# Retention and soft mixture of experts on one core: the second expert layer and the results in parts of 256, 128 and 128 columns instead of two parts of 256

## The chip, the core and the metric

The kernel runs on one core of a Trainium2 chip. The core has a matrix engine (TensorE, PE in the profile; its weight loads are a row of their own, PEld), VectorE (DVE), ScalarE (ACT), GpSimd (POOL) and a sequencer that issues DMAs here (SyncE, SP). All data is float32. The metric is the device time of one execution in microseconds.

## The reference, cut to what matters

```python
def _attn_ref(q, k, v):                      # B, H, S, D = 8, 8, 576, 64
    scores = scale * np.matmul(q, k.transpose(0, 1, 3, 2))
    ...                                      # decay by gamma ** (i - j), lower triangle
    return np.matmul(scores * Dmat, v)
def _moe_ref(x, phi, w1, w2):                # N, D, E, 4, F = 4608, 512, 8, 4, 1024
    logits = x @ phi                         # 32 slots: 8 experts of 4
    d = softmax(logits, axis=0)
    slot_input = (d.T @ x).reshape(E, 4, D)
    for e in range(E):
        slot_out[e] = np.maximum(slot_input[e] @ w1[e], 0.0) @ w2[e]
    c = softmax(logits, axis=1)
    return c @ slot_out.reshape(32, D)       # the result, 4608 x 512
```

The last two lines of work are the ones that the change touches: the second expert layer (times `w2`) and the final product of the combine weights `c` with the 32 slot outputs.

## The kernel before, in words

**Stages.** The 4608 tokens are 36 tiles of 128. A loop over the tiles computes retention, keeps the transposed results, and gathers the first softmax over groups of four tiles; W1 and W2 are loaded behind it in units of 128x1024 (512 KB), 41 of them into slots `ws`. Then come the first expert layer (L572) and the second one (`expert_2`), and the results. The order on every engine is the order of the code: the schedule is manual, and each engine takes its instructions in that order.

**W2 in two parts.** `PARTS` divides the 512 columns of W2, of the slot outputs and of the result into two parts of 256. One call `expert_2(k, n)` is a step: four matmuls (L626) of one expert and one half of the hidden units, side by side on four groups of 32 output partitions, that add into one accumulator `pp2[k]`, a piece of the PSUM bank `pm`. Part k takes 16 steps. The operands are plain float32, and each such matmul stands in the profile as two MATMUL records.

**Slot outputs.** `slot_out(k, fill)` copies the accumulator to SBUF (ACT, L632), adds the pieces of the experts up with one matmul by the selection matrix `delta` (L635, PE), writes the sum rounded (ACT, L636) and the remainder of the rounding for the upper 64 rows (DVE, L637) into `so`. Two calls in `fill` put other work on the engines between these steps.

**Results.** `final(k, b)` makes columns of part k for group b, four token tiles: four matmuls (L651) of 128 rows by 256 columns in the rounded type float32r, one MATMUL record each, with the four combine tiles `ct[b]` as weights and `so` as moving data; two copies of 128x512 out of PSUM by `evac`, which gives them to ACT (L611) and DVE (L613) in turn; and one DMA of 512 KB on SP's queue (L660; two of 256 KB at L655 for the first group). The PSUM banks `po` of these results are four that go round, and some of the combine tiles use them too. The buffers of the results are the free slots and W2 slots that have been read, in the list `stg`.

**Combine tiles.** `stack_c(g)` makes `ct[g]` with four transposes (L537) and one copy, on DVE (L543) for even g and on ACT (L545) for odd g.

**Order at the end.** 16 steps of part 0, `slot_out(0)` with the first two combine tiles and three steps of part 1 in it, then for eight groups: `final(0, b)`, the combine tile of group b + 2, and `STEPS[b]` steps of part 1 (2, 2, 2, 2, 2, 2, 1, 0). Then `slot_out(1)` with `final(0, 8)` in it, and the nine groups of part 1 with nothing between them. SP issues the DMAs of the results in the order in which `final` is called, and each waits for the two copies of its group.

Of the kernel before, what the change touches and what calls it, by code (L numbers as in the profile page):

```python
# [15 lines left out]
P = 128  # L16
NP = H // 2
DM = H * D
NE, NSE, F = 8, 4, 1024
NS = NE * NSE  # L20
NCH = 4
NT = 36
NG = NT // 4
# [3 lines left out]
NR = 6  # L27
CST = ((0, 64), (64, NP * 64), (64 * (NP + 1), (NCH + 1) * H), (64 * (NP + 1) + (NCH + 1) * H, (NCH + 1) * NP))
NCST = 64 * (NP + 1) + (NCH + 1) * (H + NP)
STEPS = (2, 2, 2, 2, 2, 2, 1, 0, 0)  # L30
ACT_STACKS = (3, 5, 6, 7)
PARTS = ((0, 256), (256, 512))


def tile_order():
    order = []
    for b0 in range(0, B, 2):
        for c in range(NCH):
            order.append((b0, c))
            order.append((b0 + 1, c))  # L40
        order.append((b0, NCH))
    return order
# [3 lines left out]
def retention_softmoe(ctx, tc, tok, phi, wun, cst, gtab, msel, out):  # L46
    nc = tc.nc
# [41 lines left out]
    unit_tile = {}  # L89
# [266 lines left out]
    for t in range(NT):  # L356
# [37 lines left out]
        if late and t:  # L394
            x, y = late.pop(0)
# [26 lines left out]
    def pbank():  # L422
        return ps_o.tile([P, 512], F32, name="po")
# [55 lines left out]
    for i in range(4):  # L479
        nc.tensor.matmul(pr[i * NS:(i + 1) * NS, 0:1], lhsT=en[:, i * NS:(i + 1) * NS],  # L480
                         rhs=tri[:, 63:64], start=True, stop=True, skip_group_check=True)
# [3 lines left out]
    for z in range(2):  # L485
        for i in range(4):
            nc.tensor.matmul(pph[z][i * NS:(i + 1) * NS, 0:256], lhsT=en[:, i * NS:(i + 1) * NS],
                             rhs=xN[4 * g + i][:, 2 * z:2 * z + 2], start=True, stop=True,
                             skip_group_check=True)
        if z == 0:  # L490
# [3 lines left out]
            out=acc[:, z * 256:(z + 1) * 256], in0=acc[:, z * 256:(z + 1) * 256], scalar=alpha,  # L494
# [36 lines left out]
    def stack_c(g, eng=nc.vector):  # L531
        if eng is nc.vector:
            pc = ps_n.tile([P, NP, P], F32R, name="pn")
        else:
            pc = pbank4().bitcast(F32R)
        for i in range(4):
            nc.tensor.transpose(pc[:, i, :], cs[g][:, i].rearrange("p r w s -> p (r w s)"), identr)  # L537
        if g < NR:
            c = ring.tile([P, NP, P], F32R, name="x")
        else:  # L540
            c = ctw[g - NR]
        if eng is nc.vector:
            nc.vector.tensor_copy(out=c, in_=pc)  # L543
        else:
            nc.scalar.copy(out=c, in_=pc)  # L545
        ct[g] = c
# [19 lines left out]
    for n in range(8):  # L566
        nh, eh, kp = n // 4, n // 2 % 2, n % 2
        for c in range(2):
            for i in range(4):
                w = unit_tile[(0, 4 * eh + i, nh, kp)]  # L570
                w = w[c] if isinstance(w, tuple) else w[:, c * 512:(c + 1) * 512]
                nc.tensor.matmul(p1[nh][i * NS:(i + 1) * NS, :], lhsT=sim[kp][:, c, 4 * eh + i, :],  # L572
                                 rhs=w, start=(n % 4 == 0 and c == 0),
# [3 lines left out]
        for i in range(4 if n != 2 else 0):  # L577
            w = unit_tile[(0, 4 * eh + i, nh, kp)]
# [7 lines left out]
        if n == 2:  # L586
            hm = [slots.tile([P, 1024], F32, name="kv3").rearrange("p (c e s) -> p c e s", c=4, e=NE)]
# [11 lines left out]
        if n in (5, 6):  # L599
            for i in (free[1:3], free[3:6])[n - 5]:  # L600
                x = slots.tile([P, 2, 4, 2, 2, NS], F32R, name=f"ws{i}")
# [4 lines left out]
    stg = [ws[i] for i in free[6:]]  # L606
    ev = [0]

    def evac(o, i):
        if ev[0] % 2 == 0:  # L610
            nc.scalar.copy(out=o, in_=i)  # L611
        else:
            nc.vector.tensor_copy(out=o, in_=i)  # L613
        ev[0] += 1

    pp2 = {}

    def expert_2(k, n):
        lo, hi = PARTS[k]
        fh, e = divmod(n, NE)  # L620
        if n == 0:
            pp2[k] = pm[:, 0:hi - lo]
        u = unit_tile[(1, e, k, fh)]
        w = u.rearrange("p (c f) -> p c f", c=4)
        for i in range(4):
            nc.tensor.matmul(pp2[k][i * NS:(i + 1) * NS, :], lhsT=hm[fh][:, i, e, :], rhs=w[:, i, :],  # L626
                             start=(n == 0), stop=(n == 2 * NE - 1), skip_group_check=True)
        stg.append(u)

    def slot_out(k, fill):  # L630
        lo, hi = PARTS[k]
        nc.scalar.copy(out=p2s[:, lo:hi], in_=pp2[k])  # L632
        fill[0]()
        pso = ps_n.tile([P, NP, P], F32, name="pn").rearrange("p a i -> p (a i)")[:, 0:hi - lo]
        nc.tensor.matmul(pso, lhsT=delta, rhs=p2s[:, lo:hi], start=True, stop=True)  # L635
        nc.scalar.copy(out=so[:, lo:hi], in_=pso)  # L636
        nc.vector.tensor_tensor(out=so[64:P, lo:hi], in0=pso[64:P], in1=so[64:P, lo:hi].bitcast(F32),  # L637
                                op=ALU.subtract)
        fill[1]()

    def final(k, b):
        lo, hi = PARTS[k]
        w = hi - lo
        o = stg.pop(0)
        stg.append(o)
        o = o[:, 0:4 * w].rearrange("p (c f) -> p c f", c=4)
        n = 512 // w
        for c0 in range(0, 4, n):
            po = pbank().rearrange("p (c f) -> p c f", c=n)
            for c in range(c0, c0 + n):  # L650
                nc.tensor.matmul(po[:, c - c0, :], lhsT=ct[b][:, c, :], rhs=so[:, lo:hi],  # L651
                                 start=True, stop=True)
            evac(o[:, c0:c0 + n, :], po)
            if k == 0 and b == 0:
                nc.sync.dma_start(  # L655
                    out=out[0, :, c0 * w:(c0 + n) * w].rearrange("p (c f) -> p c f", c=n),
                    in_=o[:, c0:c0 + n, :])
        if k == 0 and b == 0:
            return
        nc.sync.dma_start(out=out[k * NG + b].rearrange("p (c f) -> p c f", c=4), in_=o)  # L660

    for n in range(2 * NE):
        expert_2(0, n)
        if n == 1:
            hidden_out(1)
        if n in (3, 5, 7, 9):
            split_c(n // 2 + 4)
# [2 lines left out]
        stack_c(0)  # L670
        stack_c(1, nc.scalar)

    def fill_1():
        for n in range(3):
            expert_2(1, n)

    slot_out(0, (fill_0, fill_1))
    n = 3
    for b in range(NG - 1):
        final(0, b)  # L680
        if b + 2 < NG:
            stack_c(b + 2, nc.scalar if b % 2 else nc.vector)
        for _ in range(STEPS[b]):
            expert_2(1, n)
            n += 1
    slot_out(1, (lambda: final(0, NG - 1), lambda: None))
    for b in range(NG):
        final(1, b)
    man.close()


# [21 lines left out]

def unpack(o):
    import numpy as np
    o = o.reshape(2, NG, P, 4, 256).transpose(1, 3, 2, 0, 4).reshape(NT, P, DM)
    y = np.empty((B, S, DM), o.dtype)
    for t, (b, c) in enumerate(tile_order()):
        if c < NCH:
            y[b, c * P:(c + 1) * P] = o[t]  # L720
        else:
            y[b:b + 2, NCH * P:] = o[t].reshape(2, 64, DM)
    return y.reshape(B * S, DM)
# [72 lines left out]
```

## Time and profile before

| | us |
|---|---|
| time, median of 3 runs (range) | 234.79 (234.09 to 235.82) |
| time of the profiled execution | 233.35 |
| span of the profiled execution | 231.6 |
| first result matmul of part 0 | 199.6 |
| first result matmul of part 1 | 215.9 |
| last copy of a result out of PSUM ends | 223.0 |
| SP's last wait, for the result DMAs, ends | 230.5 |

The times in the span count from its start. PE is busy for 215.7 us of it (93%), DVE for 130.4, ACT for 82.4, POOL for 62.5. The DMA engines move 72.54 MB, of which 9.44 MB are the results. In the profile a group of instructions is one line with its count, its busy time and the mean duration of one; a matmul's duration covers its way through the array, so the distance between the starts of two matmuls is shorter than the duration of one. The granted TensorE clock of the run is 0.984 on average, and 1.00 in the windows from 200.7 to 223.0 us.

### The profile page before, as it was taken

The page shows a single profiled execution, that of the slowest core. Times are in us where ns is not written, and L with a number is a line of the kernel's source. Part 1 is how long each engine was busy: PE and PEld are TensorE (multiplying, and loading weights), DVE is VectorE, ACT ScalarE, POOL GpSimd, SP SyncE. Part 2 cuts the span into 40 slices and gives each one's busy share as a digit, 9 for nine tenths or more (in the row PEclk, how much of TensorE's full clock was granted, in tenths as well). Part 3 has the DMA queues.
Part 4 walks back from the last instruction along what each step waited for, and adds up shares of the span by engine and source line. Part 5 has one row for each costly group of instructions (what it writes and reads, how often), then busy time and mean ns, then how long its engine had stood idle before and what let it go on. Part 6 is the DMA issues. An engine that isn't in the chain of part 4 may idle for free.

```text
span 231.6 us, 9098 instructions
## 1 busy us (share of the span) xinstructions
PE 215.7 (93%) x3971; PEld 159.7 (69%) x3971; DVE 130.4 (56%) x302; ACT 82.4 (36%) x198; POOL 62.5 (27%) x72
## 2 busy tenths in 40 slices
PE   8789999999999999999999999999899999999730
PEld 8678877777886886787887787887763245666620
DVE  0365645766756767746847855864764132446740
ACT  2231542452443433442352352353131142444730
POOL 2743414334233333515313531440100110000000
PEclk9999999999999999999999999999999999999985
DMA  7999898789899799899789998887573899666897
GB/s 228 392 382 325 317 339 303 253 327 403 282 333 378 260 311 381 311 343 335 257 297 363 345 380 297 293 296 248 181 276 126 326 415 408 256 246 267 356 404 290
DMA packets 23511, 72.54 MB, mean 313 GB/s; under 512 B 2608, under 2 KB 2992, under 8 KB 23472
## 3 DMA queue, kind: packets, MB, share of 16 engines
q1 hardware_dynamic: 23184, 71.51, 84.1%
q8 instruction: 31, 0.51, 0.9%
q10 hardware_dynamic: 288, 0.46, 0.6%
q14 instruction: 8, 0.07, 0.1%
HBM read 62.52 MB, written 9.44 MB: 311 GB/s over the span
## 4 chain that ended last, share of the span: by engine, by line
PE 89%; DVE 4%; ACT 2%; issue 1%; DVEq 0%
PE px L234 14%; PE pss L195 13%; PE pn L263 8%; PE pst L255 7%; PE px L222 7%; PE pn L180 7%; PE pm L626 6%; PE pm L277 5%; PE pm L325 4%; PE po L651 4%; PE pst L572 3%; PE pn L572 3%; PE px L131 2%; DVE sT L200 2%; DVE sT L203 1%
## 5 line engine op out<-in xcount | busy, mean ns | idle before, releaser
L155 POOL TENSOR_TENSOR kv<-kv,cst 128x512 f32<-128x512 f32 x36 | 37.5, 1042 | 85.0 <-DMA kv<-in_tok 72.4
L241 DVE TENSOR_TENSOR x<-px,gb 128x512 f32<-128x512 f32 (+1 forms) x37 | 24.9, 675 | 31.9 <-PE px L234 30.9
L234 PE MATMUL px<-sT,kv 128*64 128x128 f32 x576 | 38.6, 275 | 2.6 <-DVE sT L203 1.8
L200 DVE TENSOR_TENSOR sT<-pss,cst 64x256 f32<-64x256 f32 x72 | 30.3, 421 | 10.9 <-PE pss L195 8.5
L181 ACT COPY kt<-pn 128x512 f32<-128x512 f32 x36 | 21.1, 587 | 40.7 <-PE pn L180 40.7
L234 PEld LDWEIGHTS px<-sT,kv 128*64 128x64 f32 x576 | 30.9, 137 | 4.6 <-PE pst L255 2.3
L265 ACT COPY x<-pn 128x512 f32<-128x512 f32 x33 | 19.3, 585 | 36.7 <-PE pn L263 36.6
L195 PE MATMUL pss<-qs,kt 64*64 64x64 f32 (+1 forms) x1152 | 31.6, 247 | 0.7 <-ACT kt L181 0.7
L195 PEld LDWEIGHTS pss<-qs,kt 64*64 64x64 f32 x1152 | 26.1, 133 | 6.9 <-issue 4.6
L255 PEld LDWEIGHTS pst<-kv 128*64 128x64 f32 x512 | 17.5, 137 | 10.1 <-issue 7.9
L180 PE MATMUL pn<-ident,kv 128*128 128x128 f32 x144 | 22.7, 280 | 0.4 <-DMA kv<-in_tok 0.4
L203 DVE TENSOR_TENSOR sT<-pss,cst 128x512 f32<-128x512 f32 x32 | 22.1, 692 | 0.9
L255 PE MATMUL pst<-kv 128*64 128x64 f32 x512 | 21.9, 228 | 0.0
L263 PE MATMUL pn<-ident,x 128*128 128x128 f32 x132 | 21.7, 287 | 0.1
L163 POOL TENSOR_TENSOR gb<-g,cst 128x512 f32<-128x512 f32 x16 | 16.6, 1040 | 10.9 <-DVE x L241 10.9
L222 PE MATMUL px<-qs,sb 64*64 64x128 f32 (+1 forms) x512 | 18.8, 267 | 0.0
L180 PEld LDWEIGHTS pn<-ident,kv 128*128 128x128 f32 x144 | 16.1, 141 | 2.0 <-DMA kv<-in_tok 0.5
L263 PEld LDWEIGHTS pn<-ident,x 128*128 128x128 f32 x132 | 13.8, 141 | 4.4 <-issue 2.6
L613 DVE COPY ws<-po 128x512 f32<-128x512 f32 x18 | 12.0, 689 | 8.6 <-PE po L651 8.2
L258 ACT COPY sb<-pst 128x256 f32<-128x256 f32 x32 | 11.8, 368 | 13.1 <-PE pst L255 12.6
L222 PEld LDWEIGHTS px<-qs,sb 64*64 64x64 f32 x512 | 12.4, 132 | 4.7 <-DVE sT L200 3.4
L611 ACT COPY ws<-po 128x512 f32<-128x512 f32 x18 | 10.5, 588 | 11.0 <-PE po L651 10.9
(153 smaller groups left out, 221.8 us busy)
## 6 DMA issues: line engine op xcount, KB each, us to landing
ws<-in_w SPq DMA_DIRECT2D x57, 512.0 KB, 6.2
kv<-in_tok SPq DMA_DIRECT2D x35, 512.0 KB, 5.8
qs<-in_tok SPq DMA_DIRECT2D x36, 256.0 KB, 4.6
out<-ws SPq DMA_DIRECT2D x17, 512.0 KB, 3.7
kv<-in_w SPq DMA_DIRECT2D x4, 512.0 KB, 5.5
kv<-in_tok SPq DMA_DIRECT2D x2, 256.0 KB, 4.0
qs<-in_w SPq DMA_DIRECT2D x2, 256.0 KB, 6.3
out<-ws SPq DMA_DIRECT2D x2, 256.0 KB, 2.2
```

What stands on the lines that cost most here:

```text
L155: nc.gpsimd.tensor_tensor(out=v, in0=v, in1=vt[:, c, :].unsqueeze(2).broadcast_to([P, H, D]), op=ALU.mult)
L180: nc.tensor.transpose(pk[:, a, :], k[:, 2 * a:2 * a + 2, :].rearrange("p j d -> p (j d)"), ident)
L181: nc.scalar.copy(out=kt, in_=pk)
L195: nc.tensor.matmul(ps[r, j, a, cols], lhsT=kt[e, a, r], rhs=q[e, a, cols], start=True, stop=True, skip_group_check=True)
L200: nc.vector.tensor_tensor(out=s[r, :, aa, 0:64], in0=ps[r, :, aa, 0:64], in1=tri[r].unsqueeze(1).unsqueeze(2).broadcast_to([D, 2, 2, 64]), ...
L203: nc.vector.tensor_tensor(out=s[:, :, :, 64:P], in0=ps[:, :, :, 64:P], in1=gm.unsqueeze(1).broadcast_to([P, 2, NP, 64]), op=ALU.mult)
L222: nc.tensor.matmul(px[r, j, a // 2, cols], lhsT=sb[i if c == NCH else b % 2][e, a, :], rhs=qT(t)[e, a, cols], start=(i == 0 and a < 2), st ...
L234: nc.tensor.matmul(px[al * D:(al + 1) * D, j, z, :], lhsT=v[:, 2 * a + j, :], rhs=s[:, j, a, :], start=(c == 0 and z == 0), stop=True, ski ...
L241: nc.vector.tensor_tensor(out=xv[:, j], in0=px[:, j, 0:2], in1=g[:, j], op=ALU.mult)
L255: nc.tensor.matmul(pst[j * D:(j + 1) * D, a, :], lhsT=k[:, 2 * a + j, :], rhs=v[:, 2 * a + j, :], start=(c == 0 and a == 0 and b % 2 == 0) ...
L263: nc.tensor.transpose(pn[:, a, :], xT[t][:, a, :], ident)
L265: nc.scalar.copy(out=x, in_=pn)
```

## The change

The second part of 256 columns becomes two parts of 128 columns; the first part keeps its 256. The loads and the units of W2 in memory stay as they are: parts 1 and 2 read the two halves of each chunk of the same units.

```diff
-STEPS = (2, 2, 2, 2, 2, 2, 1, 0, 0)
+STEPS = (0, 2, 0, 3, 0, 3, 0, 2)
-PARTS = ((0, 256), (256, 512))
+PARTS = ((0, 256), (256, 384), (384, 512))
...
     def expert_2(k, n):
         lo, hi = PARTS[k]
+        h = lo // 256
...
-        u = unit_tile[(1, e, k, fh)]
+        u = unit_tile[(1, e, h, fh)]
...
-            nc.tensor.matmul(pp2[k][i * NS:(i + 1) * NS, :], lhsT=hm[fh][:, i, e, :], rhs=w[:, i, :],
+            nc.tensor.matmul(pp2[k][i * NS:(i + 1) * NS, :], lhsT=hm[fh][:, i, e, :],
+                             rhs=w[:, i, lo - h * 256:hi - h * 256],
                              start=(n == 0), stop=(n == 2 * NE - 1), skip_group_check=True)
-        stg.append(u)
+        if hi == (h + 1) * 256:
+            stg.append(u)
...
     def final(k, b):
...
-        o = stg.pop(0)
-        stg.append(o)
-        o = o[:, 0:4 * w].rearrange("p (c f) -> p c f", c=4)
         n = 512 // w
+        if k == 0 or b % 2 == 0:
+            o = stg.pop(0)
+            stg.append(o)
+            open_tile[0] = o
+        o = open_tile[0]
+        if k:
+            o = o[:, b % 2 * 512:(b % 2 + 1) * 512]
+        ov = o.rearrange("p (c f) -> p c f", c=4)
...
-        if k == 0 and b == 0:
-            return
-        nc.sync.dma_start(out=out[k * NG + b].rearrange("p (c f) -> p c f", c=4), in_=o)
+        if k == 0 and b:
+            nc.sync.dma_start(out=out[b], in_=o)
+        if k and b == NG - 1:
+            nc.sync.dma_start(out=out[2 * NG - 1, :, (k - 1) * 512:k * 512], in_=o)
+        elif k and b % 2:
+            nc.sync.dma_start(out=out[NG + (k - 1) * 4 + b // 2], in_=open_tile[0])
...
-    def fill_1():
-        for n in range(3):
-            expert_2(1, n)
-
-    slot_out(0, (fill_0, fill_1))
-    n = 3
+    done = {1: 0, 2: 0}
+
+    def steps(k, n):
+        for i in range(done[k], done[k] + n):
+            expert_2(k, i)
+        done[k] += n
+
+    slot_out(0, (fill_0, lambda: steps(1, 6)))
     for b in range(NG - 1):
         final(0, b)
         if b + 2 < NG:
             stack_c(b + 2, nc.scalar if b % 2 else nc.vector)
-        for _ in range(STEPS[b]):
-            expert_2(1, n)
-            n += 1
-    slot_out(1, (lambda: final(0, NG - 1), lambda: None))
+        steps(1, STEPS[b])
+    slot_out(1, (lambda: final(0, NG - 1), lambda: steps(2, 4)))
+    for b in range(6):
+        final(1, b)
+        if b % 2:
+            steps(2, 4)
+    slot_out(2, (lambda: final(1, 6), lambda: [final(1, b) for b in (7, 8)]))
     for b in range(NG):
-        final(1, b)
+        final(2, b)
```

A group of part 1 or 2 is now four matmuls of 128 columns, all in one PSUM bank, and one copy of 128x512. Two groups share a buffer of 512 KB and one DMA; the ninth group of each part has a DMA of 256 KB (lines of 2 KB). The number of copies out of PSUM stays at 36, and the bytes of the results stay the same, in another order that the host undoes.

On PE, between the first groups of part 0 (`pm` is the accumulator of the steps, `kt` the slot outputs, the rows with `gb_2960` are the transposes of a combine tile). Before:

```order
L537 MATMUL pn<-gb_2960,ws_3075 128x128 x4
L626 MATMUL pm<-ws_99,kv_3023 32x256 x4
L626 MATMUL pm<-ws_100,kv_3023 32x256 x4
L651 MATMUL po<-kt,x 128x256 x4
L537 MATMUL po<-gb_2960,ws_3075 128x128 x4
```

With the change (L627 is L626 of before, and L659 is L651):

```order
L537 MATMUL pn<-gb_2960,ws_3075 128x128 x4
L659 MATMUL po<-kt,x 128x256 x4
L537 MATMUL po<-gb_2960,ws_3075 128x128 x4
L627 MATMUL pm<-ws_102,kv_3023 32x128 x4
L627 MATMUL pm<-ws_103,kv_3023 32x128 x4
```

The steps of 128 columns stand only behind every second group, six instead of three of them have run earlier, and ten instead of thirteen are left for these groups.

On PE, from the last group of part 0 on. Before:

```order
L651 MATMUL po<-kt,acc 128x256 x4
L635 MATMUL pn<-qs_3072,qs_2694 128x256
L651 MATMUL po<-kt,x 128x256 x24
L651 MATMUL po<-kt,gb_3028 128x256 x4
L651 MATMUL po<-kt,g_3029 128x256 x4
```

With the change (`kt` in the middle is the sum of part 1):

```order
L659 MATMUL po<-kt,acc 128x256 x4
L638 MATMUL pn<-qs_3072,qs_2694 128x128
L627 MATMUL pm<-ws_96,kv_3023 32x128 x4
L627 MATMUL pm<-ws_97,kv_3023 32x128 x4
L627 MATMUL pm<-ws_98,kv_3023 32x128 x4
L627 MATMUL pm<-ws_99,kv_3023 32x128 x4
L659 MATMUL po<-kt,x 128x128 x8
L627 MATMUL pm<-ws_100,kv_3023 32x128 x4
```

Where nothing stood behind L635, four steps of part 2 stand now behind L638, and then two groups of part 1 alternate with four steps.

On DVE, where the third part's slot outputs are made (L640 is L637 of before):

```order
L613 COPY ws_128<-po 128x512
L613 COPY ws_129<-po 128x512
L640 TENSOR_TENSOR kt<-pn,kt 64x128
L613 COPY ws_130<-po 128x512
L613 COPY ws_132<-po 128x512
```

This third L640 is new. The copy behind it, into `ws_130`, is that of `final(1, 7)`; the copies of `final(1, 6)` and `final(1, 8)` are ACT's.

More of the change, by code (lines that the diff above doesn't have):

```diff
@@ L652, in final @@
                                  start=True, stop=True)
-            evac(o[:, c0:c0 + n, :], po)
+            evac(ov[:, c0:c0 + n, :], po)
             if k == 0 and b == 0:
@@ L656, in final @@
                     out=out[0, :, c0 * w:(c0 + n) * w].rearrange("p (c f) -> p c f", c=n),
-                    in_=o[:, c0:c0 + n, :])
-        if k == 0 and b == 0:
-            return
-        nc.sync.dma_start(out=out[k * NG + b].rearrange("p (c f) -> p c f", c=4), in_=o)
+                    in_=ov[:, c0:c0 + n, :])
+        if k == 0 and b:
[4 more added lines that the diff above has]
+            nc.sync.dma_start(out=out[NG + (k - 1) * 4 + b // 2], in_=open_tile[0])
+    open_tile = [None]
     for n in range(2 * NE):
@@ L715, in unpack @@
     import numpy as np
-    o = o.reshape(2, NG, P, 4, 256).transpose(1, 3, 2, 0, 4).reshape(NT, P, DM)
+    x = np.empty((NG, 4, P, DM), o.dtype)
+    x[..., 0:256] = o[0:NG].reshape(NG, P, 4, 256).transpose(0, 2, 1, 3)
+    for k in range(2):
+        f = slice(256 + k * P, 256 + (k + 1) * P)
+        y = o[NG + k * 4:NG + k * 4 + 4].reshape(4, P, 2, 4, P).transpose(0, 2, 3, 1, 4)
+        x[0:8, :, :, f] = y.reshape(8, 4, P, P)
+        x[8, :, :, f] = o[2 * NG - 1].reshape(P, 2, 4, P)[:, k].transpose(1, 0, 2)
+    o = x.reshape(NT, P, DM)
     y = np.empty((B, S, DM), o.dtype)
```

## The prediction

> **What bounds the kernel now.** I read the end of the span first. The DMA issues of SP in time order, who SP waits for, and the busy time by stretch:
>
> ```profile
> 217.47 9.18 SPq L660 DMA_DIRECT2D out<-ws  x9
> ...
> SPq L660 <- DVE ws L613: 4.4, 6, 2.0
> SPq L792 <- DMA out<-ws: 3.8, 1, 3.8
> ...
> core 0: us, PE busy (x) PEld busy (x) DVE busy (x) ACT busy (x) POOL busy (x), PEclk, DMA share, GB/s
> 200.70:215.90 15.20, 14.25 (x162) 9.20 (x154) 8.65 (x14) 6.82 (x13) 0.00 (x0) 1.00 0.67 263
> ...
> 219.00:229.00 10.00, 3.00 (x19) 2.30 (x18) 3.70 (x6) 2.92 (x5) 0.00 (x0) 0.75 1.02 405
> ```
>
> The first row is the nine DMAs of part 1: issued from 217.47 to 226.65, after which SP waits 3.8 us more, to 230.5. From 219 to 229 the DMA engines are full (share 1.02, 405 GB/s) while PE works 3 of 10 us. So the end is a drain at 405 GB/s: 512 KB (524,288 bytes) take 1.295 us. The first of the nine waited 2.0 us for DVE's copy (the longest in the second row), so the queue was empty then, and the end is
>
> 217.47 + 9 x 1.295 + 1.4 = 230.5,
>
> where 1.4 us (issue to first byte, last byte to SP's wait) is what is left over. The nine DMAs cannot start before part 1 has slot outputs. In the stretch before, 200.7 to 215.9, the DMA engines are at 0.67 and PE is busy for 14.25 of 15.20 us: there PE is the bound. The chain of waits says what it does:
>
> ```profile
> 201.60 0.67 PE po L651 x4
> 202.26 0.29 PE po L537 x4
> 202.56 1.00 PE pm L626 x16
> ...
> 213.40 0.59 ACT ws L611
> 213.98 0.28 ACT qs L632
> 214.26 0.04 issue
> 214.31 0.71 PE pn L635 x2
> 215.02 0.02 issue
> 215.04 0.38 ACT kt L636
> 215.42 0.02 issue
> 215.45 0.44 DVE kt L637
> 215.89 0.04 issue
> 215.93 1.70 PE po L651 x10
> ```
>
> A group of part 0 takes 0.67 + 0.29 + 1.00 = 1.96 us for 512 KB, more than the 1.295 us of its DMA. Then, from 214.3 to 215.9, PE waits for the slot outputs of part 1.
>
> So the question is when the last results that PE makes *late* reach SP, and how many DMA units of 1.295 us stand behind that point.
>
> **The prices.** For steps and result matmuls:
>
> ```profile
> 198.20 1.43 PE pm L626 x24
> ...
> 59.46 1.08 PE pm L277 x32
> ...
> L626 PE MATMUL pm<-ws,kv 128*32 128x256 f32 x128 | 8.1, 383 | 0.0
> ...
> L277 PE MATMUL pm<-x,phs 128*32 128x128 f32 x288 | 11.2, 276 | 0.0
> ...
> 215.93 1.02 PEld L651 LDWEIGHTS po<-kt,x 128*128 128x128 f32 x8 [1.33 <-DVE kt L637]
> ...
> 172.48 0.52 PEld L513 LDWEIGHTS pn<-qs,acc 128*128 128x128 f32 x4 [0.41 <-DVE et L498]
> ...
> L651 PEld LDWEIGHTS po<-kt,x 128*128 128x128 f32 x48 | 6.4, 188 | 4.7 <-issue 2.5 <-DVE kt L637 1.3 <-ACT ws L611 0.8
> ...
> L513 PEld LDWEIGHTS pn<-qs,acc 128*128 128x128 f32 x4 | 0.5, 190 | 0.4 <-DVE et L498 0.4
> ```
>
> *Steps of 128 columns.* L277 has their exact shape (128 rows, 32 outputs, 128 columns, float32, four side by side): 32 records, four steps' worth, take 1.08 us. By duration, one pass is 383 - 276 = 0.107 us shorter than at 256 columns, two passes to a step. Two steps of 256 columns take 1.00, so two of 128 take 1.00 - 4 x 0.107 = 0.57, three 0.79, four about 1.0 (between 0.57 + 0.43 and L277's 1.08), six 1.5. Three steps before took 1.43: the six in the first slot_out stand in the place of these at no cost. All 32 steps together cost what 16 did.
>
> *Result matmuls of 128 columns.* No row shows a float32r product of 128 moving columns. The one of 256 is paced by its weights: eight loads in 1.02 us, the last of them 0.188, so one per (1.02 - 0.19)/7 = 0.119. L513 has the same 128x128 weights with only 32 moving columns: (0.52 - 0.19)/3 = 0.11. Halving the columns therefore saves next to nothing; I take 0.115, 0.46 us for a group of one part. The bounds are 0.07 (four float32r transposes on the chain in 0.29) and 0.22 (two passes of 0.107, as plain float32). Nearest is L513, the same weight load with less to stream.
>
> *Entry.* 0.67 on the chain against 4 x 0.119 = 0.48: a group behind steps pays 0.20 to load its first weights, one behind transposes does not (I take half of this where 128 columns follow).
>
> **Part by part.** *Part 0.* Groups 0, 2, 4, 6 follow steps: 4 x (0.67 + 0.29) = 3.84. Groups 1, 3, 5, 7 follow transposes: 4 x (0.47 + 0.29) = 3.04, less 0.29 since group 7 has none. Ten steps in runs of 2, 3, 3, 2: 0.57 + 0.79 + 0.79 + 0.57 = 2.72. From 199.6 this is 9.3, to 208.9. The copies do not stop it:
>
> ```profile
> L613 DVE COPY ws<-po 128x512 f32<-128x512 f32 x18 | 12.0, 689 | 8.6 <-PE po L651 8.2
> ...
> L611 ACT COPY ws<-po 128x512 f32<-128x512 f32 x18 | 10.5, 588 | 11.0 <-PE po L651 10.9
> ```
>
> DVE has three copies in two groups, 2.07 us, and PE needs 2.3 to 2.5. A group's DMA now comes every 1.2 us on average; at 1.295 each the queue falls about 2 us behind, and has caught up when part 1's first DMA comes.
>
> *slot_out(1).* final(0, 8) 0.67, the sum matmul 0.36 (half of L635's 0.71), four steps 1.0: PE at 211.0. The slot outputs are there by then: from 209.9, a cast 0.28 and a subtraction 0.31 (I scale 0.38 and 0.44 down with their columns). The 1.6 us of PE's wait are filled; were the steps not there, it would wait about 0.7. So part 1 begins at 211.0, 4.9 earlier than before.
>
> *Part 1.* Two groups 0.92 + 0.1 entry, four steps 1.0: 2.0 us for each 512 KB. The copy lands 0.85 after PE (matmul tail, DVE's 0.69): DMAs at 212.9, 214.9, 216.9. The last four steps end at 217.0. Then the new chain: the copy by ACT 0.3, final(1, 6) and the sum matmul to 218.0; on ACT the copy of final(1, 6), to 218.4, stands ahead of the cast 0.28; on DVE the subtraction 0.31 stands ahead of the copy of final(1, 7), 0.69. So that pair's DMA comes at 219.7, with final(1, 8)'s 256 KB beside it.
>
> *Part 2.* PE is free at 218.9 and the slot outputs are there; groups every 0.46 give 512 KB every 0.92, less than 1.295. So from 219.7 on the DMA engines are never short again.
>
> *The end.* 219.7 + (1 + 0.5 + 4 + 0.5) x 1.295 + 1.4 = 219.7 + 7.8 + 1.4 = 228.9 against 230.5: 1.6 us less. The profiled execution took 233.35 (span 231.6), so 231.75 by its own time; set against the median of 234.79 I take off 1.5, since the second slot_out chain has more hand-overs than I counted, and forecast **233.3**. The change starts part 1 five microseconds earlier and gives nearly all of it back: 36 more result matmuls at 0.115 are 4.1 us of PE.
>
> **The rivals.** A run like this tells about 1%, 2.35 us, from no change.
>
> *A, the short product is cheaper.* If loads ran ahead as they do for the transposes (0.07 each), part 1's pairs take 1.65 and the tail starts 1 us earlier: 2.5 us off, 232.3. For it: those transposes are float32r of 128 columns. Against it: their loads are shorter, and L513's 0.11.
>
> ```profile
> L537 PEld LDWEIGHTS pn<-gb,ws 128*128 128x128 f32 x20 | 2.0, 140 | 0.4 <-issue 0.4
> ...
> L537 PE MATMUL pn<-gb,ws 128*128 128x128 f32 x20 | 2.4, 240 | 0.0
> ```
>
> By the Trainium skill, page "TensorE: Matmul & The Clock Gate", section "Back-to-back issue gap", a stream of load and matmul pairs of 128 columns runs at about 81 ns each; by that the sum would be an estimated 232.5, on this rival's side. L513's 0.11 us, with fewer columns, disagrees with it here.
>
> *B, the short product is dearer, and the kernel slower.* If float32r loses its single fast pass at 128 columns and costs 0.22, each group of parts 1 and 2 costs 0.42 more. Part 1's four pairs end 3 us later, and part 2, 9 x 0.88 = 7.9 from 222, outruns the DMA no longer: its last copy ends at 230.9, and 0.65 + 1.4 for the last 256 KB gives 233.0: 2.5 to 3 us over before, 237.5. By the same sum it turns slower than before from about 0.17 for a product, and by 1% from 0.20. For it: no row has such a product, and plain float32 takes 0.107 a pass at this width. Against it: the transposes in float32r show 240 ns against the 276 of plain float32 at 128 columns, so the type keeps its rate there.
>
> *C, the tail does not move.* If the third slot_out keeps DVE and ACT for longer than summed, final(1, 7)'s copy comes at 220.9 and the end is the old one. That needs 1.2 us in a chain of 2.7; it is within the forecast's neighbours, not a case with a sign of its own.
>
> **How the numbers follow.** The sum has 0.56, C 0.04, A 0.15, B 0.25. The likeliest alone spans 232.3 to 234.6. The range takes in most of A and the half of B that is nearest: 231.8 to 237.0. Faster by over 1%: A and a little of the sum's edge, 0.16; slower by over 1%: B, 0.24; within: 0.60.
>
> **What would show it.** Each step right or wrong in the changed profile: L659 groups of 128 columns on the chain at 0.46 (A: 0.3, B: 0.9); runs of four steps at 1.0; the first product of part 1 at 211.0; SP's first DMA of part 1 at 212.9 and the fourth at 219.7, with the DMA engines full from there on; SP's last wait ending at 228.9. I would be wrong if PE showed gaps behind L638, if the copies set the pace in part 0, or if the DMA engines were not full after 220.

## The result, and the profile after

Over 20 runs each the change has a median of 232.84 us (231.37 to 235.60) against 234.47 us (232.83 to 237.11) for the kernel before. The ratio is 0.9946, with a 95% interval of 0.9921 to 0.9971: by it 1.3 us faster (by the two medians 1.6) where 1.5 was forecast, and within the 1% of no change that the prediction named. Ratios here and below are taken over the fast runs of a kernel, those within 1.5% of its fastest; two of the profiles below (the wait alone; parts of 256, 176 and 80) are of slower runs, but the granted clock is 1.00 in them too while PE makes the results.

The profiled execution of the change took 234.41 us, its span is 232.6 us, one us *longer* than that of before. Two spans are not to be compared here. The first result matmul of part 0 starts at 199.56 us in the profile before and at 201.93 after, although the code ahead of it is the same but for six short steps in the place of three long ones:

```profile
199.56 0.74 PE L651 MATMUL po<-kt,x 128*128 128x256 f32 x4
201.93 0.74 PE L659 MATMUL po<-kt,x 128*128 128x256 f32 x4
```

In the 13 profiles besides the one before it lies between 199.0 and 203.6. The scatter of the runs' times is of that size too. So all that follows counts from the start of the first result matmul of part 0 to the end of SP's last wait for the DMAs. I call this stretch the **end stretch**: 30.96 us before, 29.65 after, 1.31 us less. It is taken from the starts and ends of the trace, one profile for each kernel.

SP's issues after the change in time order, and who SP waits for:

```profile
203.08 0.82 SPq L663 DMA_DIRECT2D out<-ws  x2
204.65 8.92 SPq L667 DMA_DIRECT2D out<-ws  x8
215.51 7.14 SPq L671 DMA_DIRECT2D out<-ws  x4
222.74 0.38 SPq L669 DMA_DIRECT2D out<-ws  x1
223.35 3.78 SPq L671 DMA_DIRECT2D out<-ws  x4
227.22 1.15 SPq L669 DMA_DIRECT2D out<-ws  x1
```

```profile
SPq L671 <- DVE ws L613: 7.5, 4, 2.3
SPq L817 <- DMA out<-ws: 3.2, 1, 3.2
```

The third row of the issues is part 1: four pairs from 215.51 to 222.65, each waiting for DVE's copy, up to 2.3 us. The fourth row is the 256 KB of part 1's ninth group, the last two rows are part 2. SP's last issue ends at 228.37, and 3.2 us later its wait, at 231.57; less 201.93 this is 29.64. The DMA engines just before the late pair's bytes move, and in the last stretch:

```profile
core 0: us, PE busy (x) PEld busy (x) DVE busy (x) ACT busy (x) POOL busy (x), PEclk, DMA share, GB/s
222.00:223.00 1.00, 1.00 (x12) 1.00 (x10) 0.94 (x2) 0.43 (x2) 0.00 (x0) 1.00 0.00 0
...
224.00:230.00 6.00, 1.82 (x17) 1.68 (x16) 2.07 (x3) 1.39 (x3) 0.00 (x0) 0.75 1.02 402
```

They stand still in the microsecond from 222, and from 224 on they are full, at 402 GB/s, as in the drain before. The fourth of the pairs, the late one, by itself:

```profile
222.32 0.33 SPq L671 DMA_DIRECT2D out<-ws  x1
```

The chain of waits of the change has the rest in order of time:

```profile
202.00 0.67 PE po L659 x4
202.66 0.29 PE pn L537 x4
202.96 0.55 PE po L659 x4
...
203.80 0.57 PE pm L627 x16
...
212.66 1.01 PE pm L627 x32
213.68 1.04 PE po L659 x8
...
218.81 1.01 PE pm L627 x32
219.82 0.61 PE po L659 x4
220.43 0.02 issue
220.45 0.59 ACT ws L611
221.04 0.18 ACT kt L639
221.22 0.02 issue
221.24 0.30 DVE kt L640
221.54 0.04 issue
221.59 4.25 PE po L659 x36
```

A result group costs 0.67 behind steps (202.00) and 0.55 behind transposes (202.96). Two steps of 128 columns cost 0.57, four 1.01. The row at 212.66 stands where PE waited before. Two groups of part 1 take 1.04, and the nine groups of part 2, 36 products in one run, 4.25 with the end of the last one. From start to start a product of 128 columns takes 0.113 (the 36 starts lie within 3.96 us). At 220.45 the new hand-over shows: ACT's copy of final(1, 6), ACT's cast, DVE's subtraction.

### The profile page after: what moved, and what is told of

It is laid out like the page before. It is cut to its first block, busy times and chain, and to the rows that moved or that the text cites. A ratio compares the mean times of both kernels' runs of the same rounds, so it can differ in the third digit from the quotient of the medians.

```text
span 232.6 us, 9432 instructions
## 1 busy us (share of the span) xinstructions
PE 218.5 (94%) x4137; PEld 166.6 (72%) x4137; DVE 131.4 (57%) x303; ACT 82.8 (36%) x200; POOL 62.5 (27%) x72
## 4 chain that ended last, share of the span: by engine, by line
PE 88%; DVE 4%; DMA 3%; issue 1%; SPq 1%; ACT 0%; DVEq 0%
PE px L234 14%; PE pss L195 12%; PE pn L263 8%; PE pst L255 7%; PE px L222 7%; PE pn L180 7%; PE pm L627 7%; PE po L659 6%; PE pm L277 4%; PE pm L325 4%; PE pst L572 3%; PE pn L572 3%; DMA kv<-in_tok 3%; DVE sT L200 2%; DVE sT L203 1%
## 5 line engine op out<-in xcount | busy, mean ns | idle before, releaser
L195 PE MATMUL pss<-qs,kt 64*64 64x64 f32 (+1 forms) x1152 | 32.4, 248 | 1.5 <-issue 0.9
L265 ACT COPY x<-pn 128x512 f32<-128x512 f32 x33 | 19.3, 585 | 38.5 <-PE pn L263 38.4
L258 ACT COPY sb<-pst 128x256 f32<-128x256 f32 x32 | 11.7, 367 | 12.7 <-PE pst L255 12.2
```

Source lines behind the costliest of these rows:

```text
L195: nc.tensor.matmul(ps[r, j, a, cols], lhsT=kt[e, a, r], rhs=q[e, a, cols], start=True, stop=True, skip_group_check=True)
L265: nc.scalar.copy(out=x, in_=pn)
```

## The experiments

Three questions were open. Is it the division that gains, or the new order of the steps, or the filled wait? Is the short product on the path, and in which part? Do the DMA engines or PE set the end? All ratios are to the kernel before, with 95% intervals.

**The wait alone.** Two parts; only slot_out(1) is filled more.

```diff
-    for b in range(NG - 1):
+    for b in range(NG - 2):
         final(0, b)
...
-    slot_out(1, (lambda: final(0, NG - 1), lambda: None))
+    slot_out(1, (lambda: final(0, NG - 2), lambda: final(0, NG - 1)))
```

> Two parts of 256 as before; only the wait for the slot outputs of part 1 gets more work: final(0, 7) and final(0, 8) stand in slot_out(1) instead of final(0, 8) alone. Counted from the first result matmul of part 0 to the end of SP's last wait, before has 30.9 us and the change 29.6. Drain theory (the end is the first late DMA plus the DMA units behind it at 1.295 us; whatever starts part 1 earlier moves the end as far, and no more): one group's 0.65 us goes into the wait, part of it is lost to the copies ahead on DVE, so 0.5 us less, 30.4. Rival, the wait of 1.6 us is all there is to gain and the division only fills it: 29.6 to 29.9, as much as the change brought.

Measured: 30.58, ratio 0.9964 (0.9926 to 1.0002). Filling the wait is worth 0.4 us here, not 1.3. It does more for PE than for the end: part 1's first product comes 15.42 us after the first result matmul on the chain (219.10 less 203.68), where it took 16.30 before. But the DMA engines are still busy with part 0 when part 1's first DMA is issued, at 220.63 (share 1.03 from 219.5 to 220.5), and that DMA lands 3.3 us later, where part 1's first DMA took 2.7 in the kernel before. So 0.5 of the 0.88 us is lost in the queue.

**The order alone.** Two parts; the steps come in longer runs.

```diff
-STEPS = (2, 2, 2, 2, 2, 2, 1, 0, 0)
+STEPS = (0, 4, 0, 4, 0, 4, 0, 1, 0)
```

> Two parts of 256 as before; only the order of the steps is that of the change: 4, 4, 4 and 1 steps behind groups 1, 3, 5 and 7 instead of 2 behind each of six groups and 1 behind the seventh. Drain theory with the entry cost of 0.20 us per run of steps: three runs fewer, and the first weights of the transposes' successors are loaded ahead: 0.6 to 1.1 us less, 29.8 to 30.3. Rival, only the division into smaller parts moves the end: 30.9, no change.

Measured: 29.87, ratio 0.9900 (0.9854 to 0.9946). That one line brings 1.09 of the change's 1.31 us. Its chain shows how:

```profile
199.08 0.67 PE po L651 x4
199.75 0.29 PE pn L537 x4
200.04 0.55 PE po L651 x4
200.59 0.30 PE po L537 x4
200.90 1.86 PE pm L626 x32
202.76 0.67 PE po L651 x4
...
212.25 0.71 PE po L651 x4
212.96 0.45 PE pn L635 x2
```

Four steps of 256 columns in one run take 1.86, where two runs of two took 2 x 1.00 before; and the group that now follows transposes takes 0.55 in the place of 0.67. One run less is 0.14 + 0.12 = 0.26 us, and three runs of seven are gone: 0.8 of the 1.09. The rest is at the sum matmul L635. On the chain before, two copies of ACT (0.59, of a result of group 7, and 0.28, of the accumulator) stand ahead of L635, which then takes 0.71; here it follows group 8 at once and takes 0.45.

**Both, and the second once more.**

```diff
-STEPS = (2, 2, 2, 2, 2, 2, 1, 0, 0)
+STEPS = (0, 4, 0, 4, 0, 4, 0, 0, 0)
...
-        for n in range(3):
+        for n in range(4):
...
-    slot_out(1, (lambda: final(0, NG - 1), lambda: None))
+    slot_out(1, (lambda: final(0, NG - 2), lambda: final(0, NG - 1)))
```

> Two parts of 256, with both: four steps in slot_out(0), runs of 4 behind groups 1, 3 and 5, and final(0, 7) and final(0, 8) in slot_out(1). Drain theory: both savings act on the start of part 1, about 1.1 to 1.4 us less than before, 29.5 to 29.8, so that two parts come to about what three do. Rival, the smaller parts are what counts: 30.9 to 30.4, well behind the change.

Measured: 29.51, ratio 0.9933 (0.9901 to 0.9965). Two parts in this order are where the change is, 0.14 us ahead of it, with no division. Part 1 now starts 2.14 us earlier than before (14.16 after the first result matmul on the chain), but only 1.45 of it reach the end: the DMA engines are full from 214 us on, and part 1's first DMA is not issued until 216.16.

```profile
215.00:228.00 13.00, 5.64 (x36) 4.45 (x34) 6.14 (x10) 5.17 (x9) 0.00 (x0) 0.82 1.02 405
```

From there on an earlier start of part 1 gains nothing; the last DMA that finds the queue empty is one of part 0. The kernel with the order alone was then run a second time:

> The two parts of 256 columns with the batched steps once more, since its first ratio to before, 0.990 (0.985 to 0.995), is further down than its 1.09 us from the first result matmul to the last wait explain. Theory (the order alone is worth about 1.1 us, and the time ahead of the first result matmul scatters by itself): the stretch is 29.8 to 29.9 again and the ratio about 0.995, as the change's. Rival (the order also shortens something ahead of the results): the ratio stays at 0.990 and the first result matmul starts before 199.5 again.

Measured: 29.87 again, ratio 0.9967 (0.9931 to 1.0003), first result matmul at 199.68. The end stretch repeats to the hundredth, and the two ratios of the same kernel, 0.990 of six runs and 0.997 of ten, show how little such a ratio can tell here.

**The division with the steps spread.** Three parts, the steps in short runs: eight in part 0, where the kernel before had seven and the change four, and six in part 1, where the change has three. The filled slot_out(1) stays.

```diff
-STEPS = (0, 2, 0, 3, 0, 3, 0, 2)
+STEPS = (2, 2, 1, 1, 1, 1, 1, 1)
...
         final(1, b)
-        if b % 2:
-            steps(2, 4)
+        steps(2, 2)
```

> The change's three parts with the steps spread as before's two parts have them: 2, 2, 1, 1, 1, 1, 1, 1 behind the groups of part 0 and 2 behind each of the first six groups of part 1. Counted from the first result matmul of part 0 to the end of SP's last wait (30.96 before, 29.65 the change). Theory of the order (a run of steps costs its entry, about 0.2 us, whatever its length, and the gain of the change is that it has half as many runs; the division by itself gives back what it brings): four runs more in part 0 and three more in part 1, 1.5 us over the change, 31.2, no better than before. Rival (the division is the gain): at most 0.3 over the change, 29.9.

Measured: 31.46, ratio 1.0064 (1.0026 to 1.0103). The division in this spread order is *slower* than before, by 0.5 us in the end stretch, so the division does not bring the gain by itself. Its chain has the same steps in shorter runs:

```profile
204.94 0.35 PE pm L627 x8
205.29 0.67 PE po L659 x4
...
213.52 0.59 PE po L659 x4
214.11 0.57 PE pm L627 x16
```

One step takes 0.35, two 0.57, four 1.01, so a run costs 0.13 + 0.22 for each step; and every group stands behind steps, at 0.67 and 0.59. The 0.5 us hang on this placing: ten steps in five runs of two, as the kernel before has them, would be three runs fewer, an estimated 0.75 us at 0.25 a run, and so a little ahead of the kernel before. That order was not run.

**The short products.** In one part each, four products of 128 columns become two of 256; half of the token tiles of that part are left out.

```diff
-            po = pbank().rearrange("p (c f) -> p c f", c=n)
-            for c in range(c0, c0 + n):
+            pb = pbank()
+            po = pb.rearrange("p (c f) -> p c f", c=n)
+            if k == 1:
+                for c in (0, 2):
+                    nc.tensor.matmul(pb[:, c * P:c * P + 256], lhsT=ct[b][:, c, :], rhs=so[:, 128:384],
+                                     start=True, stop=True)
+            for c in range(c0, c0 + n if k != 1 else c0):
```

> The change, but in part 1 each group has two result matmuls of 256 columns in the place of four of 128 (two of the four token tiles are left out and the columns are others, so the results of part 1 are not the reference's); copies and DMAs stay. This halves the extra weight loads of part 1. Theory (the 0.115 us of a short product is on the path in part 1, where PE is the bound): nine groups cost 0.24 instead of 0.46, seven of them stand ahead of the late pair, so that pair comes 1.2 to 1.5 us earlier and the end with it: 28.2 to 28.4 us from the first result matmul, against 29.6. Rival (the short products hide behind the copies and the DMAs): 29.6.

Measured: 28.37, ratio 0.9913 (0.9874 to 0.9953): 1.28 us less than the change. The short products of part 1 are on the path: up to the late pair's first group 14 products are gone, 0.09 us for each. The same for part 2 (`k == 2`, columns 256 to 512 of `so`):

> The same in part 2: two matmuls of 256 columns in the place of four of 128 (results of part 2 not the reference's), copies and DMAs as in the change. PE's last 4.2 us become about 2.2 to 3. Theory (from the fourth pair of part 1 on the DMA engines are the bound): no change of the end, 29.4 to 29.7. Rival (PE's last matmul and its copy set the end): about 1.3 to 2 us less, 27.6 to 28.3.

Measured: 29.63 against 29.65, ratio 0.9953 (0.9918 to 0.9988). There they hide.

**The DMAs of part 2**, halved (the last one, of 256 KB, likewise):

```diff
...
-            nc.sync.dma_start(out=out[NG + (k - 1) * 4 + b // 2], in_=open_tile[0])
+            m = 1024 if k == 1 else 512
+            nc.sync.dma_start(out=out[NG + (k - 1) * 4 + b // 2, :, 0:m], in_=open_tile[0][:, 0:m])
```

> The change, but the DMAs of part 2 write only the first group of each pair and half of the last 256 KB (the other half of part 2 is not written); matmuls and copies stay. Theory: of six units that are left behind the late pair, 2.25 go, 2.9 us, until PE bounds the end: 26.7 to 27.2. Rival (PE sets the end): 29.4 to 29.6.

Measured: 27.08, ratio 0.9835 (0.9771 to 0.9900), 2.57 us less. With the run before, this says that the DMA engines, not PE, are the bound of the change from part 1's last pair on.

**The fill of slot_out(1)**, taken out:

```diff
-    slot_out(1, (lambda: final(0, NG - 1), lambda: steps(2, 4)))
+    slot_out(1, (lambda: final(0, NG - 1), lambda: None))
...
-            steps(2, 4)
+            steps(2, (5, 5, 6)[b // 2])
```

> The change without the four steps of part 2 in slot_out(1): they go behind groups 1, 3 and 5 of part 1 (5, 5 and 6 steps). Theory: PE waits 0.6 to 0.8 us for the slot outputs of part 1, and all behind it, the late pair too, is later by this: 30.2 to 30.4 from the first result matmul. Rival (the filled wait of 1.6 us is what the change gains): the whole gain and more is gone, 30.9 to 31.2. Rival (the wait costs nothing, as the DMA engines still work off part 0): 29.6.

Measured: 30.47, ratio 0.9995 (0.9956 to 1.0033), 0.82 us over the change and just outside the expectation. Where the change's chain has steps, this one has a wait:

```profile
209.84 0.73 PE po L659 x4
210.57 0.02 issue
210.59 0.69 DVE ws L613
211.28 0.03 issue
211.31 0.31 DVE kt L640
211.62 0.04 issue
211.66 1.11 PE po L659 x8
```

PE makes the sum matmul L638, from 210.39 to 210.77, and then stands until 211.66, 0.89 us, longer than I reckoned: the copy of final(0, 8) is ahead of the subtraction on DVE. The run says something of the division too: division and order without the fill take 30.47, 0.60 us more than the order alone (29.87). In this order the division pays only with the steps that it leaves to fill this wait.

**Other places and sizes.** First the change's parts with the late pair moved out of slot_out(2)'s hand-over:

```diff
-STEPS = (0, 2, 0, 3, 0, 3, 0, 2)
+STEPS = (0, 3, 0, 4, 0, 4)
...
-    slot_out(1, (lambda: final(0, NG - 1), lambda: steps(2, 4)))
-    for b in range(6):
+    slot_out(1, (lambda: final(0, 6), lambda: [final(0, 7), final(0, 8), steps(2, 4)]))
+    for b in range(7):
         final(1, b)
-        if b % 2:
+        if b in (2, 4, 6):
             steps(2, 4)
-    slot_out(2, (lambda: final(1, 6), lambda: [final(1, b) for b in (7, 8)]))
+    slot_out(2, (lambda: final(1, 7), lambda: final(1, 8)))
```

> The change's three parts of 256, 128 and 128, with other places for the slot outputs: 5 steps in slot_out(0), runs of 3, 4 and 4 behind groups 1, 3 and 5, final(0, 6) to final(0, 8) in slot_out(1) with the four steps behind them; runs of four behind groups 2, 4 and 6 of part 1, and final(1, 7) and final(1, 8) in slot_out(2). The late pair, final(1, 6) and final(1, 7), then no longer waits with its copy behind the subtraction of slot_out(2). Drain theory: the end comes 0.9 to 1.4 us earlier than the change's, 28.3 to 28.7 from the first result matmul. Rival (PE's sum sets the end; it is the same but for one run of steps): 29.3 to 29.6.

Measured: 28.96, ratio 0.9939 (0.9904 to 0.9974): 0.7 us less than the change in the end stretch, and 0.3 outside the expectation.

```profile
218.25 0.69 DVE L613 COPY ws<-po 128x512 f32<-128x512 f32 x1 [1.35 <-PE po L659]
219.00 0.33 SPq L671 DMA_DIRECT2D out<-ws  x1
...
221.08 3.01 SPq L671 DMA_DIRECT2D out<-ws  x4
```

The late pair is issued 19.59 us after the first result matmul (219.00 less 199.41), 0.80 before that of the change. Its copy follows PE's product at once, where in the change it begins 0.47 us behind it (221.56, the product ends at 221.09); the other 0.36 us are PE's, which has the products ready sooner in this order. And here the queue runs dry once more: the DMA share is 0.27 from 219 to 220, part 2's first pair is issued only at 221.08, and the drain counts from that. Most of the 0.3 us was missed here.

Then the change with parts of 256, 192 and 64 columns (the copies and DMAs of `final` follow the widths, as the expectation says; their lines are not shown):

```diff
-PARTS = ((0, 256), (256, 384), (384, 512))
+PARTS = ((0, 256), (256, 448), (448, 512))
```

> The change with parts of 256, 192 and 64 columns instead of 256, 128 and 128. The number of result matmuls and their order stay, the copies grow from 36 to 45, the DMAs of part 1 are 384 KB a group, those of part 2 256 KB a pair. Drain theory: part 1 now makes 384 KB in about 0.8 us of PE on average, nearly as fast as its DMA of 0.97 us, so the DMA engines stay full from part 0 on and only 2.25 units are left for part 2, which PE bounds: 2 us less than the change, 27.6 (bounds 27.0 to 28.5). Rival, PE and its weight loads bound the end in the change too (last copy plus a constant): PE's sum is the same, so 29.6, no gain.

Measured: 28.54 (to the last of SP's waits), ratio 0.9929 (0.9891 to 0.9968). It is 1.1 us less than the change and the shortest of all with the whole result, yet just outside the 27.0 to 28.5 that were expected. The DMA engines are full, at a lower rate:

```profile
224.00:230.00 6.00, 2.34 (x21) 2.23 (x20) 1.27 (x3) 1.18 (x4) 0.00 (x0) 0.77 1.02 386
```

386 GB/s with lines of 3, 2 and 1 KB, against 402 with 4 KB in the change. Half of the results, 4.72 MB, take 12.2 us at 386 GB/s and 11.7 at 405, so the rate explains an estimated 0.6 of the 0.9 us by which 27.6 was missed; the rest stays open. And parts of 256, 176 and 80, as differences from the kernel just shown:

```diff
-PARTS = ((0, 256), (256, 448), (448, 512))
+PARTS = ((0, 256), (256, 432), (432, 512))
-STEPS = (0, 2, 0, 3, 0, 3, 0, 2)
+STEPS = (0, 3, 0, 3, 0, 3, 0, 3)
...
-    slot_out(0, (fill_0, lambda: steps(1, 6)))
+    slot_out(0, (fill_0, lambda: steps(1, 4)))
```

> Parts of 256, 176 and 80 columns, four steps in slot_out(0) and runs of three behind groups 1, 3, 5 and 7; otherwise as the kernel of 256, 192 and 64, which took 28.6 us from the first result matmul to its last DMA's end where 27.6 was expected: its DMA engines were full from early on, but at 380 to 396 GB/s, with lines of 3 and 2 KB, where lines of 4 KB reach 405. Theory (PE hides now, DMA lines set the end): lines of 2.8 and 2.5 KB, 28.2 to 28.8, no better than 192 and 64. Rival (the smaller last part gave PE's price away): 0.4 us better, 28.2 or less.

Measured: 29.19, ratio 0.9924 (0.9894 to 0.9954). Not better than 192 and 64, and outside the expectation. Its rate is lower again, with the DMA engines at 0.99:

```profile
224.00:230.00 6.00, 2.73 (x25) 2.61 (x24) 1.61 (x4) 1.70 (x4) 0.00 (x0) 0.82 0.99 379
```

The steps are placed otherwise too, so what of the 0.65 us between these two kernels is the rate was not separated. By time alone none of the kernels between 0.990 and 0.997 is told from another; only the end stretches rank them, and only one kernel's was taken twice.

## Why the prediction was right, point by point

- **The drain.** The end is where part 1's late pair comes, plus the DMA units behind it. Forecast, from the first result matmul (199.56 there): fourth pair at 20.1 us, end at 29.3. Measured: 222.32 - 201.93 = 20.4, and 29.65. Halving part 2's matmuls moved nothing and halving its DMAs 2.57 us, so the mechanism is shown, not only its number.
- **PE's sum.** Forecast: part 1 begins at 11.4 us, its first DMA at 13.3, part 2 at 19.3. Measured: 11.7 (213.68 less 202.0 on the chain), 13.6, 19.7. All are late by 0.3 to 0.4, and this is where 1.6 us less became 1.31. The term is the group behind transposes: I took 0.47, it takes 0.55, in four groups 0.32 us. I had put the whole of a group's entry down to the steps ahead of it. (I took off 1.5 and not the sum's 1.6, for hand-overs in the second slot_out chain that I might not have counted. That chain took 2.50 us, from 219.82 to 222.32, where the sum had 2.7. That the margin brought the forecast nearer was luck.)
- **The short product.** 0.113 from start to start against the 0.115 that I took; 36 of them 4.25. *Rival A* (0.07) and *rival B* (0.22) both fell. The reason to choose, the weight load of L513, held: the loads of the short products come every (1.41 - 0.19)/11 = 0.111 us, as those of L513 do (0.11). The Trainium skill, page "TensorE: Matmul & The Clock Gate", section "Back-to-back issue gap", has about 81 ns for load and matmul pairs of 128 columns and names no type there; these float32r pairs take 113 ns, so the measurement decides.
- **The steps.** Forecast 0.57, 0.79 and 1.0 for two, three and four; the chain has 0.57, 0.79 and 1.01.
- **slot_out(1).** I put the price of the unfilled wait at 0.7 us; taking the fill out cost 0.82.
- **The queue behind part 0.** Here the prediction was wrong, without effect. The queue was to have caught up when part 1's first DMA comes, but that DMA landed 3.6 us after its issue, the third and the late pair 2.6: about 1 us of part 0 still stood ahead of it. Two pairs later the queue had caught up. (That it falls 2 us behind did not follow from the prediction's own terms: eight groups, at 1.16 us of PE against 1.295, make 1.1. The trace does have 2: part 0's last DMA landed 4.6 us after its issue.)
- **What the prediction did not see** is which edit earns the 1.3 us. It had the entry cost as a term, and named as the gain that part 1 starts five us earlier, nearly all given back by the short products. The sum was right and the credit was not worked out: the same batching in two parts brings 1.09 us with no division, and with the filled wait 1.45, more than the change's 1.31. To the order alone the division adds 0.22 us with its fill and costs 0.60 without; with the steps spread it ends 0.50 behind the kernel before. *Rival C* did not come; but its place, the copy of final(1, 7) behind the subtraction, is real: out of it, the copy begins 0.43 us sooner behind its product.

## What to carry to other kernels

When a change has several edits, price and run each alone: here the division moved the end by between 0.2 us less and 0.6 us more, as it was combined, and its companion, a reordered table of numbers, took off more than one. Where a program ends in a drain, find the last transfer that finds the queue empty; only what delays that one, and the bytes behind it, counts. Each gain can move that point to another transfer, as two of the runs here show, and then the next gain pays less. And a last part that is small in bytes is of use only as long as the parts ahead keep the queue full. Compare short effects in a stretch with its own start, not in spans that carry the scatter of everything ahead.

## What the runs showed of the hardware that was not expected

A float32r product keeps its duration in the profile, whose matmul ends are modelled, when its columns are halved. The groups by shape of the change (busy time, mean ns), a run of weight loads from its timeline, and of the kernel before the least, median and greatest duration of the 256 columns:

```profile
L659 PE MATMUL po<-kt,x 128*128 128x128 f32 x48 | 6.2, 280 | 0.0
L659 PE MATMUL po<-kt,x 128*128 128x256 f32 x24 | 4.4, 303 | 0.0
L537 PE MATMUL pn<-gb,ws 128*128 128x128 f32 x16 | 1.8, 237 | 0.0
```

```profile
221.59 1.41 PEld L659 LDWEIGHTS po<-kt,x 128*128 128x128 f32 x12 [0.19 <-DVE kt L640]
```

```profile
L651 PE MATMUL po<-kt,x x48: 278/281/389, 199.6 to 219.9; 128*128 128x256 f32 x48
```

280 ns at 128 columns. The 256 columns have a mean of 303 here, since the first of each group is longer (up to 389 in the kernel before, where the median is 281). A float32r transpose of 128 columns has 237. The distance from one product to the next hardly changes with the columns either: 0.113 us at 128 columns, 0.119 at 256, and for the 32 columns of L513 0.11. That the weight load sets this pace fits all three; no run changed the load alone.

Going from steps of 32 outputs, four side by side, to products of 128 outputs and back costs 0.13 + 0.12 us each time: 0.13 is what a run of steps takes besides its steps (0.35, 0.57 and 1.01 for one, two and four), 0.12 what a group takes more behind steps than behind transposes (0.67 and 0.55). Together this is more than a whole step of 128 columns, 0.22.

The result DMAs in lines of 4 KB drained at 402 to 405 GB/s, in lines of 3 to 1 KB at 386, of 2.8 and 2.5 KB at 379, with shares of 1.02, 1.02 and 0.99. The kernel with part 2's DMAs halved, in lines of 2 KB, had 381 at 1.03 (223 to 226 us). The line length is the likely cause; the kernels differ in more than that.
